# A delta-rule attention and an MLP on one core: the written order of the first five steps is replaced

## The chip, the core and the metric

The kernel runs on one core of a Trainium2 chip. The core has five engines with an instruction queue each: TensorE (PE, matrix products), VectorE (DVE), ScalarE (ACT), GpSimd (POOL) and SyncE (SP, which here only issues DMAs). Each engine works through its own queue in the order in which the instructions were written; a semaphore holds an instruction until what it needs is done, and everything behind it on that engine then waits too. The metric is the device time of one execution in microseconds; smaller is better. The kernel before took 668.8 us (median of three: 668.42, 668.8 and 674.51).

## The reference

The first half is a delta-rule recurrence for 4 batches and 8 heads of width 48 over 768 positions; the second an MLP over the 3072 resulting rows of 384, with 2048 hidden units and a hard-swish.

```python
k_n = k / (np.linalg.norm(k, axis=-1, keepdims=True) + 1e-06)
for t in range(S):
    y[:, :, t] = np.einsum('bhd,bhde->bhe', q[:, :, t], state)
    v_old = np.einsum('bhde,bhd->bhe', state, kt)
    state = state + bt[:, :, :, None] * np.einsum('bhd,bhe->bhde', kt, vt - v_old)
...
x = np.ascontiguousarray(attn_out.transpose(0, 2, 1, 3)).reshape(B * S, H * D)
h = x @ w_in
g = h * np.clip(h + 3.0, 0.0, 6.0) / 6.0
return g @ w_out
```

`w_in` (384 x 2048) and `w_out` (2048 x 384) arrive in 64-bit floats, so they have to be converted on the chip.

## The kernel before

**Steps.** The 768 positions are cut into 24 steps of 32. A step treats 4 batches x 32 positions on the 128 partitions, for all 8 heads. Steps are joined in groups: step 0 alone, then 1 to 4, 5 to 8 and so on. Two steps make a block of 256 rows for the MLP.

**One step t, in the kernel's names.** `prep` (word `p`): normalized keys `kb` (L510, POOL), transposes of keys and queries (`pt`, L524, PE), their copy to `KQ` (L532, ACT), the products of keys with keys and queries (`sc`, L547, PE), and the two masked products `L` and `LB` (L558, DVE). `norms` (`n`): squares (L407 on ACT, L409 on POOL), sum (L413), root (L417) and reciprocal, for `kb`. `mask` (`m`, L486) and `scaled` (`b`, L498): products with beta on POOL.

A triangular system has to be inverted for each step. Step 0 has it by products (`x0`, L596 to L656, DVE, PE and ACT by turns). Steps 1 to 4 have theirs by a substitution on DVE (`i1`: transpose `A` at L469, then pairs of small products L730 and L735, transpose to `X` at L473), which yields two halves for each step, joined by `x1` to `x4` (L694 to L710, products `pi` at L684). Steps 5 to 8 have it by the longer substitution `i2` (L469, L759, L764, L473).

`chain` (`h`) is the recurrence: state products `ks` (L806, PE), `R` (L901, L909, DVE), `pz` (L827, PE), its copy to Z (L927, ACT), state products `su` (L938, PE), the new state (L956, DVE). `output` (`y`): `y` from `ks` (L843 on ACT, L819 on DVE), `py` (L827, PE), sum (L863, DVE; L861 on ACT for step 0), transpose `yt` (L873, PE) and copy to `xT` (L877, ACT).

**Weights.** `w` loads one of 16 chunks of raw weights, 768 KB each (L331, SP); the first 8 are of `w_in`, the last 8 of `w_out`. `a` is one of the four scale steps of a chunk on ACT (L356), `c` one of its three conversions on DVE (L378, L383, L389). The chunks share a few raw buffers, so a later load waits until an earlier chunk has been read.

**MLP.** `ua` and `ub` are the projections of the two halves of block 0 (`ph`, L994), `u` the units of the later blocks (`ph` again, and `po` at L1155); `ra`, `rb`, `ru` are the first half of the activation on ACT (L1001), `ga`, `gb`, `gu` the second on DVE (L1004). `e` copies a finished `po` out. A projection needs `xT` and the converted chunks of `w_in`; `po` needs `g` and `w_out`.

**What sets the order.** `ORDER` is a string of words, one for each piece of such work; `x0*3` stands for three pieces. `do` runs the generator that a word names up to its next `yield`, and so the instructions of that piece are written next, on whichever engines they belong to. `k`, `q`, `v` and `B` issue one load each (keys, queries, values, beta; 48 KB each, L168, L180, L193), `z` and `s` settings. When the string has been worked off, steps 5 to 23 follow by a fixed plan in a loop, which the change doesn't touch. `needs` and `ring` only assert that an order is possible and pick buffers in PSUM; semaphores come from the data.

Of the kernel before, what the change touches and what calls it, by code (L numbers as in the profile page):

```python
# [19 lines left out]


ORDER = """
k*2 B*3 k*2 n0 k*2 z B s*2 n0*6 k*2 q*2 n1 q n1 q w k p0 z*3 k n1*2 k*2 n1*2 z p0*2 s k p0*3 a k a
m0 a n2 m1 p0 x0*2 w q x0 n1 x0*3 c*2 n2 a k s p1*2 a s*2 k q s*2 x0 n2 k*2 c x0 n2 x0 w q a*4 q
p1 n2 k*2 a x0 m2 p1 c*2 p1 n2*3 b1 q b0 s p1 x0 q w x0 n2 q*2 c*3 x0 n4 k p1 k p2*2 x0*2 a*2 c
a*2 q*3 a*2 w v p3*2 q x0 q n4 p2*2 c p2 v c n4*2 a*3 z v n4 c a m3 v c p2 n4*2 q p2 k c b2 h0 c
h0 w a*2 h0 p4*2 a*2 m4 p3 q*4 h0 q k w p4*2 c*5 v*2 p3 k p3*3 k*2 p4*2 v*2 p4 m6 k a w a w i1*3 k
i1*7 a i1*2 a i1*2 v i1*2 k b3 k y0 c y0*3 ua*2 ra*2 i1*3 w v ga v a*3 i1*2 ua i1 h1 i1 q w ua ra
ua i1 ra*2 ga i1 k ua a*2 ra ga i1 ga ua ra ua ra i1 ga i1*4 ua ga n5 x1*2 k x1 c a ra v a*2 ga x2
k*2 ga*2 ua*2 x1 ra*2 x1*2 ua h1*2 n5 k ga c ra ga*2 h1 c y1*2 ua ra w ga ua ra x2 n5 ga y1*2 ua  # L30
ra ga h1 v*3 n5*2 k y1*2 ua a ra x2 ub*2 a n5 rb*2 h1 x3 ga c*2 w a h2 y2 v gb ub rb gb x2 gb ub*2
n5*2 b4 rb n5 x2*2 h2 gb rb gb m5 a n5*2 ub rb gb v c q*2 v q*5 n5 ub n5 rb gb h2 y2 c h2 q ub
y2*2 rb ub p5 b5 h2 rb gb*2 a*2 x3 p5 ub y2*2 k p5*2 h2 rb h3 p5 gb h3 ub*2 q rb gb rb gb ub a x3
p6 v c x4 x3 rb gb ub p7 rb gb y3 c*2 v c p7*2 y3 v p7*2 b6 x3 q x3 ub h3 a p6*2 c p5*2 rb gb k m7
w p6 h3 u p6 k*2 q*3 a*2 y3 a p6 c y3 v y3*2 u n9 v k q a c a c*2 u*2 ru gu w k a*2 c a*2 x4 c*2
ru p7 a gu k u a*2 p7 p6 m8 u*3 a k u*2 k h3 w ru*2 a*2 gu*2 x4 c*2 x4 k c*2 a p8 k a*2 u ru k h3
u*2 h4 ru a b8 gu k gu y4 p8*3 u h4 k*2 c q k*9 q u p8*2 k ru k*2 gu k c n9 q u q*2 p8 k*2 b7 n9*2
x4 i2 u x4 q i2*2 q ub ru gu u rb gb i2*2 h4*2 u*2 i2 ru i2*6 y4 i2 gu i2*7 u i2 ru gu i2 u*3 ru
i2*4 gu ru i2*2 v i2 c gu u*3 a u ru c i2 u*2 i2 gu i2*3 q i2*5 y4 n9 i2 e*2 n9*2 i2*4 q i2 y4 e
n9 u ru i2*3 u h4 i2 ru*2 gu h4 u n9 i2*2 u i2 e i2*6 y4 u k n9*3 u gu i2 y4 n9 i2 p9 q i2*2 gu  # L40
"""


# [1493 lines left out]
```

## Time and profile before

| | |
|---|---|
| times of three runs | 668.42, 668.8, 674.51 us |
| profiled execution | 670.31 us, span 668.6 us |
| PE busy | 635.9 us (95%) |
| DVE busy | 488.6 us (73%) |
| ACT busy | 272.7 us (41%) |
| POOL busy | 203.5 us (30%) |
| moved from and to HBM | 26.84 and 4.72 MB |

The page gives busy time and instruction counts of each engine, then the span in 40 slices of 16.7 us, where a digit is the busy share in tenths; the row PEclk is the clock that PE was granted. A table of stages gives the same in us for chosen stretches. The timeline has one row for each run of equal instructions: start, length, engine, line and operation, and in brackets how long the engine was idle before and what ended that.

### The profile page before, as it was taken

The page shows a single profiled execution, that of the slowest core. Times are in us where ns is not written, and L with a number is a line of the kernel's source. Part 1 is how long each engine was busy: PE and PEld are TensorE (multiplying, and loading weights), DVE is VectorE, ACT ScalarE, POOL GpSimd, SP SyncE. Part 2 cuts the span into 40 slices and gives each one's busy share as a digit, 9 for nine tenths or more (in the row PEclk, how much of TensorE's full clock was granted, in tenths as well). Part 3 has the DMA queues.
Part 4 walks back from the last instruction along what each step waited for, and adds up shares of the span by engine and source line. Part 5 has one row for each costly group of instructions (what it writes and reads, how often), then busy time and mean ns, then how long its engine had stood idle before and what let it go on. Part 6 is the DMA issues. An engine that isn't in the chain of part 4 may idle for free.

```text
span 668.6 us, 26778 instructions
## 1 busy us (share of the span) xinstructions
PE 635.9 (95%) x11768; PEld 578.1 (86%) x11768; DVE 488.6 (73%) x1146; ACT 272.7 (41%) x532; POOL 203.5 (30%) x320
## 2 busy tenths in 40 slices
PE   2659899999999999999999999999999999999997
PEld 2548787776689988988999999999999999999997
DVE  5889686798545687747988858988758998456353
ACT  5887579432143132232244244244244144153250
POOL 6531032002511130463164255064052241331330
PEclk9778899999999999999999999999999999999999
DMA  7888146302041030031030030020020020010000
GB/s 175 203 205 223 57 94 169 65 13 46 18 84 21 3 73 2 2 76 35 3 70 7 3 70 5 3 61 3 3 50 2 2 50 2 17 24 1 26 1 24
DMA packets 88500, 33.29 MB, mean 50 GB/s; under 512 B 80160, under 2 KB 83232, under 8 KB 88384
## 3 DMA queue, kind: packets, MB, share of 16 engines
q1 hardware_dynamic: 88128, 31.29, 21.1%
q8 instruction: 92, 1.51, 1.0%
q10 hardware_dynamic: 256, 0.30, 0.2%
q14 instruction: 24, 0.20, 0.1%
HBM read 26.84 MB, written 4.72 MB: 47 GB/s over the span
## 4 chain that ended last, share of the span: by engine, by line
PE 90%; DVE 3%; DMA 3%; SPq 1%; issue 1%; ACT 1%; ACTq 0%; DVEq 0%
PE po L1219 28%; PE ph L1065 21%; PE ph L994 16%; PE po L1155 6%; PE ks L806 4%; PE pz L827 3%; PE py L827 3%; PE pt L524 3%; PE su L938 3%; PE sc L547 2%; DMA spare<-in_moe_w_in_dram 2%; PE yt L873 1%; SPq L168 1%; PE pi L684 1%; DMA w_out<-in_moe_w_in_dram 1%
## 5 line engine op out<-in xcount | busy, mean ns | idle before, releaser
L1065 PE MATMUL ph<-xT,w_in 128*128 128x128 f32 x784 | 122.9, 278 | 0.0
L994 PE MATMUL ph<-xT,w_in 128*128 128x256 f32 (+1 forms) x576 | 117.5, 355 | 0.6 <-ACT xT L877 0.6
L1219 PE MATMUL po<-w_out,g 128*128 128x192 f32 x640 | 110.6, 326 | 0.0
L994 PEld LDWEIGHTS ph<-xT,w_in 128*128 128x128 f32 x576 | 96.2, 196 | 12.7 <-ACT xT L877 0.8
L1065 PEld LDWEIGHTS ph<-xT,w_in 128*128 128x128 f32 x784 | 103.9, 192 | 1.3 <-ACT KQ L532 0.2
L1219 PEld LDWEIGHTS po<-w_out,g 128*128 128x128 f32 x640 | 104.1, 190 | 0.2
L1030 POOL TENSOR_TENSOR g<-g 128x256 f32<-128x256 f32 x112 | 67.9, 608 | 83.2 <-ACT g L1079 78.8
L1219 PE MATMUL po<-spare,g 128*128 128x192 f32 x480 | 86.7, 332 | 0.0
L1219 PEld LDWEIGHTS po<-spare,g 128*128 128x128 f32 x480 | 77.2, 190 | 1.8
L1001 ACT ACTIVATE g<-ph,halves 128x256 f32<-128x256 f32 (+1 forms) x96 | 41.2, 436 | 75.0 <-PE ph L994 74.9
L1229 POOL TENSOR_TENSOR o<-o,u 128x192 f32<-128x192 f32 x18 | 13.1, 727 | 176.2 <-ACT o L1226 87.0
L1079 ACT ACTIVATE g<-ph 128x512 f32<-128x512 f32 x56 | 33.4, 597 | 80.4 <-PE ph L1065 77.2
L1205 DVE TENSOR_TENSOR g<-g 128x512 f32<-128x512 f32 x80 | 55.7, 717 | 5.6 <-PE po L1219 5.6
L759 DVE TENSOR_TENSOR pr<-A 128x30 f32<-128x30 f32 (+9 forms) x150 | 57.4, 383 | 2.7
L764 DVE TENSOR_TENSOR A<-A,pr 128x30 f32<-128x30 f32 (+9 forms) x150 | 55.7, 371 | 3.7
L1004 DVE SCALAR_TENSOR_TENSOR g<-g,ph 128x256 f32<-128x256 f32 (+1 forms) x96 | 34.7, 370 | 31.6 <-ACT g L1001 31.2
L356 ACT ACTIVATE spare<-spare,places 128x768 uint16<-128x768 uint16 (+1 forms) x56 | 52.5, 942 | 2.6 <-DMA kf<-in_k_dram 1.4
L1094 DVE TENSOR_TENSOR g<-ph,g 128x256 f32<-128x256 f32 x56 | 23.5, 419 | 37.7 <-PE ph L1065 25.6
L1226 ACT ACTIVATE o<-po 128x192 f32<-128x192 f32 x40 | 13.2, 330 | 83.3 <-PE po L1219 83.3
L1108 DVE SCALAR_TENSOR_TENSOR g<-o,g 128x512 f32<-128x512 f32 x56 | 40.9, 730 | 7.0 <-ACT o L1105 6.9
L1155 PE MATMUL po<-w_out,g 128*128 128x384 f32 x128 | 45.2, 491 | 0.0
L510 POOL TENSOR_TENSOR kb<-kf,inv 128x384 f32<-128x384 f32 x24 | 21.3, 891 | 78.3 <-issue 47.4
(141 smaller groups left out, 1005.1 us busy)
## 6 DMA issues: line engine op xcount, KB each, us to landing
kf<-in_k_dram SPq DMA_DIRECT2D x96, 48.0 KB, 3.1
qb<-in_q_dram SPq DMA_DIRECT2D x96, 48.0 KB, 2.8
vf<-in_v_dram SPq DMA_DIRECT2D x96, 48.0 KB, 2.1
out_dram<-o SPq DMA_DIRECT2D x92, 48.0 KB, 1.6
spare<-in_moe_w_in_dram SPq DMA_DIRECT2D x4, 768.0 KB, 5.8
w_out<-in_moe_w_in_dram SPq DMA_DIRECT2D x4, 768.0 KB, 6.3
w_out<-in_moe_w_out_dram SPq DMA_DIRECT2D x4, 768.0 KB, 6.9
spare<-in_moe_w_out_dram SPq DMA_DIRECT2D x4, 768.0 KB, 5.4
```

The costliest lines, as they stand in the source:

```text
L356: nc.scalar.activation(out=z, in_=z if n else d.bitcast(I16)[:, :, :, 3], func=func, bias=places[:, n : n + 1], scale=scale,)
L759: nc.vector.tensor_tensor(out=pv, in0=A[:, j + 1 :, j].unsqueeze(2).to_broadcast([n, w, j]), in1=A[:, j, 0:j].unsqueeze(1).to_broadcast([n ...
L764: nc.vector.tensor_tensor(out=A[:, j + 1 :, 0:j], in0=A[:, j + 1 :, 0:j], in1=pv, op=ALU.subtract)
L827: nc.tensor.matmul(ps[rows(place(b)), D * h : D * h + D], lhsT=m(h)[rows(b)], rhs=z[rows(b), D * at(h) : D * at(h) + D], start=True, stop= ...
L994: nc.tensor.matmul(ph[:, cols], lhsT=w_in[:, s, f * 128 : (f + 1) * 128], rhs=xT[:, s, cols], start=(s == 0), stop=(s == NKT - 1),)
L1001: nc.scalar.activation(out=g, in_=ph, func=ACTF.Relu, bias=half, scale=1.0 / 6.0)
L1030: nc.gpsimd.tensor_tensor(out=out, in0=a, in1=b, op=op)
L1065: nc.tensor.matmul(ph[:, n], lhsT=w, rhs=x, start=start, stop=stop, skip_group_check=True)
L1108: nc.vector.scalar_tensor_tensor(out=g, in0=r, scalar=1.0, in1=g, op0=ALU.min, op1=ALU.mult)
L1155: nc.tensor.matmul(pos[c][:], lhsT=gs[blk, f // 2][:, f % 2, c * P : (c + 1) * P], rhs=w_out[:, f, :], start=(f == 0), stop=(f == NFC - 1),)
L1205: nc.vector.tensor_tensor(out=A(f, *out, 4), in0=A(f, *a, 4), in1=A(f, *b, 4), op=op)
L1219: nc.tensor.matmul(ps[n][:], lhsT=A(f - f % 2, *a)[:, f % 2], rhs=b[:, f], start=(f == 0), stop=(f == HF - 1),)
```

## The change

Only the string `ORDER` is replaced (it is one line longer, so that line numbers of the changed kernel are one higher). It has 782 words in both kernels, and each word equally often. Its description says that the order of the first five steps on all engines was made anew by a longer search, in a model corrected on a trace, with three settings averaged.

```diff
 ORDER = """
-k*2 B*3 k*2 n0 k*2 z B s*2 n0*6 k*2 q*2 n1 q n1 q w k p0 z*3 k n1*2 k*2 n1*2 z p0*2 s k p0*3 a k a
-m0 a n2 m1 p0 x0*2 w q x0 n1 x0*3 c*2 n2 a k s p1*2 a s*2 k q s*2 x0 n2 k*2 c x0 n2 x0 w q a*4 q
-p1 n2 k*2 a x0 m2 p1 c*2 p1 n2*3 b1 q b0 s p1 x0 q w x0 n2 q*2 c*3 x0 n4 k p1 k p2*2 x0*2 a*2 c
-a*2 q*3 a*2 w v p3*2 q x0 q n4 p2*2 c p2 v c n4*2 a*3 z v n4 c a m3 v c p2 n4*2 q p2 k c b2 h0 c
-h0 w a*2 h0 p4*2 a*2 m4 p3 q*4 h0 q k w p4*2 c*5 v*2 p3 k p3*3 k*2 p4*2 v*2 p4 m6 k a w a w i1*3 k
-i1*7 a i1*2 a i1*2 v i1*2 k b3 k y0 c y0*3 ua*2 ra*2 i1*3 w v ga v a*3 i1*2 ua i1 h1 i1 q w ua ra
...
+k*4 B z B k*3 n0 s k n0 B n0 B n0*4 n1*3 q*2 n1 s*2 n1*3 q*2 w*2 z q p0*2 k m0 k*4 p0*3 z*3 p0 a*3
+z p0 x0*3 w x0*2 a*3 c*2 a p1 b0 c s x0*2 k*2 n2 a b1 c*2 q n2 k*2 a p1 n2 k w s k*2 q x0*3 s c n2
+p1 c a x0*2 n2*4 x0 n2 a p2 m2 c q a c*2 x0 k*2 m1 a s b2 p1*2 w n4 q n4 c v*3 k a*4 c p2*2 x0 v
+x0 p3 n4*2 a n4*2 w s*2 p1 q*3 p2 q p2 c n4 h0 p2 c p2 q p1 v h0 q*3 p3 p4 v a*2 v c*2 p3 p4*2 v*2
+h0*2 p3*2 m4 q*4 p4*3 a*2 k*3 m3 c k*2 a k p4 p3*2 i1*2 b4 w q i1*4 y0 i1*5 a y0*2 k y0 k i1*2 b3
+v ua i1 k ra ga i1*10 ua ra ga k h1 i1 a i1 ua a ra ga w ua ra ua ra i1 v ga i1 ua i1 ua*2 i1 ga
...
 """
```

More of the change, by code (lines that the diff above doesn't have):

```diff
@@ L28 @@
-i1*7 a i1*2 a i1*2 v i1*2 k b3 k y0 c y0*3 ua*2 ra*2 i1*3 w v ga v a*3 i1*2 ua i1 h1 i1 q w ua ra
[L29 to L39, printed above, removed]
@@ L40 @@
-n9 u ru i2*3 u h4 i2 ru*2 gu h4 u n9 i2*2 u i2 e i2*6 y4 u k n9*3 u gu i2 y4 n9 i2 p9 q i2*2 gu
+k*4 B z B k*3 n0 s k n0 B n0 B n0*4 n1*3 q*2 n1 s*2 n1*3 q*2 w*2 z q p0*2 k m0 k*4 p0*3 z*3 p0 a*3
[3 more added lines that the diff above has]
+h0*2 p3*2 m4 q*4 p4*3 a*2 k*3 m3 c k*2 a k p4 p3*2 i1*2 b4 w q i1*4 y0 i1*5 a y0*2 k y0 k i1*2 b3
@@ new lines @@
+v ua i1 k ra ga i1*10 ua ra ga k h1 i1 a i1 ua a ra ga w ua ra ua ra i1 v ga i1 ua i1 ua*2 i1 ga
+i1 ra*3 ga x1*2 ua ga c x1 ua n5 x1 ra a*2 q ra a ua w ga m5 x1 ga x3 x1 a ua v h1*2 c*2 ga ra ga
+ra k*2 c y1*2 h1 y1 ua a*3 ua c y1*3 ra*2 h1 ga c*2 q ub ga*2 a n5 ub rb*2 h1 w*2 ua ra ga ua ra
+h2 x2 v q x2 gb v n5 gb n5*2 ub*2 w x3 n5 x2 ga rb v k rb w q ub gb y2 x2 v q n5 rb ub rb n5 a
+gb*3 x2 h2 n5*3 a x2 ub*3 c rb*3 gb x4 gb*2 v h2*2 a c n5*2 p6 q y2 a ub rb y2*2 gb ub*2 rb gb
+y2*2 h2 ub*2 b6 rb x4 q ub rb q gb rb gb v*2 q gb q*4 x3 rb p5 b5 x3 h2 p6 q p6 ub k rb gb*2 p8 p5
@@ new lines @@
+a p5 c x3 p5 h3 x3 k p5 p6*2 k*2 q*2 k*3 p7 p8*2 h3 y3 k p7*2 p8*2 p7*2 k h3*2 q b8 k*2 c k v k y3
+a*2 u y3*2 u y3 a h3 k q c h3 c*3 w m6 y3 u*2 q k*2 q k*3 q ru gu a*3 c p5 p6 k u c*2 w ru gu a
+u*2 a p5 k p6 a*2 q p7 m7 p7 a ru c a gu u v a c k*2 ru h4 gu u c*2 u*2 y4 h4 p8 q c x4 ru n9 gu
+u*3 a*3 k*2 m8 p8 i2*3 w x4*2 ru gu i2*2 a c k x4 u c*2 u v b7 k ru i2 y4 i2 u i2 a i2*3 n9 a gu
+i2*3 ru gu i2 a*2 c*2 i2*4 u*3 ru*2 u gu*2 a c v i2*2 u i2*2 n9*2 u i2 ru u*2 i2 c q*2 i2 u a*2 ru
+gu n9 i2*2 q gu i2*2 h4 i2 k*2 a u c i2*6 h4 i2 u k u k n9 e n9 u k i2 e i2*2 ru gu i2 n9 i2 y4*2
@@ L41 @@
+ru e i2 u i2*3 ru h4 i2*3 e u h4 v gu u gu i2*2 u n9 u y4 n9*2 i2 u i2*4 n9 ru i2 n9 y4 i2*2 gu
+i2*2 p9
 """
```

## The prediction

> **What bounds the kernel now.** First the page: how busy each engine is, and where along the span.
>
> ```profile
> PE 635.9 (95%) x11768; PEld 578.1 (86%) x11768; DVE 488.6 (73%) x1146; ACT 272.7 (41%) x532; POOL 203.5 (30%) x320
> ...
> PE   2659899999999999999999999999999999999997
> ...
> DVE  5889686798545687747988858988758998456353
> ...
> PEclk9778899999999999999999999999999999999999
> DMA  7888146302041030031030030020020020010000
> ```
>
> TensorE (PE) is idle for 668.6 - 635.9 = 32.7 us, nearly all in the first five of the 40 slices, where its clock is also cut and the DMA engines are busiest. The table of stages says it in us (columns: stretch, busy time and instructions of PE, weight loads, DVE, ACT, POOL, then clock, DMA share, GB/s).
>
> ```profile
> 0.00:10.00 10.00, 1.82 (x8) 1.57 (x8) 5.04 (x17) 3.73 (x7) 6.57 (x31) 1.00 0.58 122
> 10.00:20.00 10.00, 5.74 (x219) 4.68 (x222) 7.01 (x19) 6.93 (x10) 6.84 (x15) 1.00 1.07 261
> 20.00:30.00 10.00, 6.28 (x255) 5.03 (x246) 8.45 (x17) 9.84 (x15) 2.38 (x2) 0.68 0.83 200
> 30.00:40.00 10.00, 5.24 (x262) 4.28 (x262) 9.39 (x28) 7.52 (x11) 5.73 (x6) 0.84 0.86 183
> 40.00:50.00 10.00, 5.97 (x210) 5.14 (x209) 8.51 (x14) 9.13 (x13) 2.65 (x6) 0.80 0.76 201
> 50.00:60.00 10.00, 9.42 (x120) 8.91 (x118) 9.31 (x34) 7.24 (x15) 0.00 (x0) 0.83 1.04 270
> 60.00:70.00 10.00, 8.31 (x310) 7.50 (x310) 9.33 (x26) 6.89 (x16) 2.14 (x4) 1.00 0.70 193
> 70.00:80.00 10.00, 8.42 (x214) 7.90 (x213) 5.12 (x13) 6.06 (x12) 0.00 (x0) 0.83 0.02 4
> ```
>
> PE is busy 51.2 of the first 80 us, so 28.8 us of idle lie there; the remaining 3.9 us are the tail. From 80 to 600 us the list of waits has none of PE's. So until about 50 us VectorE (DVE, 8.5 to 9.4 of 10) and ScalarE (ACT, up to 9.8 of 10) set the pace, and then PE. The list of PE's waits (us in total, times, longest) and four rows of the timelines name the places: the waits whose cause the profile calls "issue", ACT's y of step 0, DVE's first inverse, PE's first projection, and the last chunk of w_out on PE.
>
> ```profile
> PE su L938 <- issue: 4.2, 2, 2.3
> PE sc L547 <- ACT KQ L532: 3.7, 4, 1.7
> ...
> PE sc L547 <- issue: 1.0, 2, 0.6
> ```
> ```profile
> 49.04 0.47 ACT L861 ACTIVATE y<-py 128x384 f32<-128x384 f32 x1
> ```
> ```profile
> 47.48 1.93 DVE L469 STREAM_TRANSPOSE A<-L 128x1024 f32<-128x1024 f32 x1
> ```
> ```profile
> 50.70 3.90 PE L994 MATMUL ph<-xT,w_in 128*128 128x128 f32 x18 [0.58 <-ACT xT L877]
> ```
> ```profile
> 145.07 2.74 PE L1155 MATMUL po<-w_out,g 128*128 128x384 f32 x8
> ```
>
> 50.70 is when the first projection starts: before it PE is busy for about 25 us and idle for 25.5. Between it and 80 us only 3.3 us are idle.
>
> **The change, part by part.** Both orders have 782 words and the same number of each, so nothing is added or removed: every instruction and every DMA is moved, not bought. On PE the two programs differ in the first 1614 of 6018 matmuls and are equal from there (about 165 us on). As PE does not wait between 80 and 600 us, the change is worth the PE idle it takes from or adds to the first 165 us, and no more.
>
> I compare by running sums: in the written order of each engine I add the median duration of each instruction's row (PE's at full clock), and note how much stands ahead of a milestone (us, before / after, then its time in the trace of before):
>
> - ACT, first xT copy: 39.0 / 35.3, at 50.15. Four scale steps fewer stand ahead (24, not 28, before y of step 0), at 0.93 each.
> - DVE, A (start of the first inverse): 33.0 / 30.6, at 47.48. Five weight chunks are converted ahead of it, not six.
> - DVE, R of step 1: 48.2 / 45.2, at 63.40; y of step 1: 53.0 / 49.7, at 68.33.
> - PE, first projection: 17.9 / 17.9, at 50.70; state product ks of step 2: 37.1 / 36.5, at 76.86; ks of step 3: 48.5 / 54.7; su of step 3: 74.1 / 62.6; sc of step 8 done: 85.0 / 79.8; po of the last w_out chunk: 104.7 / 104.7, at 145.07.
> - DVE, second A: 94.1 / 87.2, at 127.86; last chunk converted: 108.4 / 109.2 ahead of it, at 142.59; second X: 125.2 / 125.2, at 160.05.
>
> *Start of the projection.* Between 20 and 50 us ACT is mostly full, so 3.7 us less ahead of xT is 3.7 us earlier, if its inputs come. The chunk for which ACT waited 1.37 us at 39.16 is now SP's 42nd transfer, not its 51st, and the values of step 0 the 41st, not the 48th. Against it, the last query piece of step 4 is the 58th, not the 53rd (5 x 0.49 us of issue, 2.5 us), and stands behind a value load that needs pz of step 0 done. An estimate along that path: X of step 0 stands as it did, at 32; the query pieces of step 2, now behind the sixth chunk, land near 33, and pz of step 0 ends at 34.9; the value load and three query pieces go out by 36.9 and land 2.8 later (the page's median), 39.7; transpose and copy (0.6) to 40.3; four scale steps (3.8), y (0.47), yt (0.55) and xT (0.49) to 45.8, 4.9 us earlier than now. DVE's sum alone gives 2.4. I take 4.0, between the two ends and nearest ACT's 3.7, since y is an ACT instruction.
>
> *From there to ks of step 2.* PE's sum is 0.6 smaller. x1's transpose stands 3.4 us less deep on DVE, so PE reaches it about as it does now (wait 0.93). New: pz and py of step 1 are neighbours; before, two blocks of projection (1.5 us) covered the copy of Z. Behind pz, ACT has two relus, the y copy (0.57) and the Z copy (0.49). Bounds: 0 (copies were early) to 1.7 (all four); I take 1.0, and behind py wait two blocks of ph, yt and su.
>
> *Steps 2 to 4.* Between ks and su of step 3 PE now has 7.9 us of work, before 25.6, and DVE between R and the state 3.1, not 20.7. Links and cover: R (0.74 + 0.62) against five groups of transposes (2.2); the Z copy (0.49) against two po (1.3); y (0.55) against two po; xT (0.49) against su (0.81). All are covered by 0.3 us or more: I take 0; with the thinnest cover gone, 0.5 each, 2 in all.
>
> *Second inverse and last w_out chunk.* A needs the mask products of step 8. From the end of sc(8) PE has 24.9 us until it needs the last chunk; DVE has 0.8 + 22.0 + 0.95 = 23.8 us, plus the 0.4 us that it idled between A and this chunk in before. Slack 0.7, where before the conversion ended at 143.5, 1.5 us early. Bounds 0 to 2; I take 0.3. The second X ended 3.1 us before its reader at 165.16 and keeps that, as both move with PE.
>
> *SP and POOL.* Key blocks of later groups move past weights on SP's queue; a late one delays POOL's kb, which PE needs only from the transposes of step 5, at a PE sum of 52. Taken at 0; up to 1.4, ACT's longest wait for a key block.
>
> **Sum:** -4.0 - 0.6 + 1.0 + 0 + 0.3 = -3.3, rounded with the clock to -3.5: a start that comes earlier leaves fewer of the half-clock stretches under it, worth a few tenths. The profiled execution took 670.31 us (span 668.6 and 1.7 around it), so it would take 666.8; it lies 1.5 above the median of the three, 668.8, and from the median the forecast is **665.3 us**.
>
> **The waits named "issue".** PE waited four times for nothing that the profile shows: 0.56 at 26.1, 0.42 at 34.7, 1.86 at 41.0 and 2.34 at 71.6, 5.2 us. Counting PE's instructions in the trace, they begin at numbers 706, 1217, 1473 and 2753, each a multiple of 256 from the next (within one), and the queue "instruction" brings 16 KB packets in these stretches: I read them as instruction refills behind the weight transfers. The long ones are followed by a stretch at half clock (clock 0.54 from 72 to 75 us). My sum leaves them as they are. [...]
>
> **Rivals.**
> 1. *DVE keeps the end of the stage.* DVE idles about 12 us between 87 and 128 us, waiting for sc and for scale steps. If these do not come earlier, the last w_out chunk stays at 143.5 and PE gains only the 1.5 us of slack: 667.3. For it: slack of 0.7 in the sums. Against: sc(8) is 5.2 us earlier in PE's order.
> 2. *All of it.* The start by the full 4.9, 0.6 of order, and the refill at 71.6 (2.34 and the half clock behind it, 3.4 / 2) hidden: -9.5, 659.3. For it: weights are asked for earlier. Against: rows of 32 small matmuls still stand close together there.
> 3. *Slower: refills.* [...] pz, py, yt and su of step 1 now stand closer, and come some 4 us earlier, while the weight transfers, which ran at 183 to 270 GB/s until 70 us, do not. Each further refill costs 2.34 and up to 1.7 of half clock, 4.0. One takes the gain away (669.3), two give 673.4. For it: all four waits lie under such transfers. Against: none fell in the 50 to 62 us stretch at 1.04 DMA share.
> 4. *Nothing moves.* The projection waits for the query pieces, now deeper in SP's queue, and starts at 50.7 again: 668.8.
>
> **Numbers.** Forecast 0.42, rival 1 0.21, rival 2 0.16, rival 3 0.15, rival 4 0.06. The range 659.0 to 671.0 takes in the first two, most of rivals 2 and 4 and the one-refill half of rival 3. A measurement of this kernel tells about 1% (6.7 us) from no change: faster by that needs under 662.1, rival 2 and the best of the forecast, 0.22; slower needs over 675.5, three refills or a stall not seen here, 0.07; within, 0.71.
>
> **What would show it.** First projection at 45.8 to 48.3; first A at 43 to 45; idle of PE in the first 80 us down to about 25; a wait of py for ACT's R of about 1 us; no PE wait between 100 and 165 us beyond 0.5. The forecast is wrong if the projection starts after 50, if waits on "issue" exceed 8 us, or if PE waits for w_out at about 141 us.

## The result and the profile after

The changed kernel took **673.75 us** (median of 20 runs, 670.61 to 677.65) against 669.15 us of the kernel before (20 runs beside them, 666.54 to 674.51): a ratio of **1.0057, 95% interval 1.0036 to 1.0079**, so 2.4 to 5.3 us slower. The forecast was 665.3 us, with a range up to 671.0; it had the wrong sign and the time lies outside the range. Ratios and intervals, here and below, leave out the few executions that took over 1.5% more than the fastest of their kernel; medians are of all.

The profiled execution of the changed kernel took 673.5 us with a span of 671.8. First its page: busy time of PE, then the 40 slices.

```profile
PE 638.2 (95%) x11768; PEld 579.1 (86%) x11768; DVE 485.2 (72%) x1146; ACT 272.2 (41%) x532; POOL 202.6 (30%) x320
...
PE   3668899899999999999999999999999999999997
...
DVE  5779758899545777747878857988748988456353
...
PEclk9988999899999999999999999999999999999999
DMA  7868345502041030032030030020020020010000
```

PE is idle for 671.8 - 638.2 = 33.6 us, before 32.7. So in these two executions the change took no idle time away (in the first 80 us it is 27.5 us, before 28.8), and one thing is new: the eighth slice (117.6 to 134.3 us) shows clock 8, where before nothing behind the fifth slice did. The table of stages has it in us, with the columns of before:

```profile
20.00:30.00 10.00, 4.84 (x179) 4.19 (x179) 8.41 (x17) 6.23 (x10) 4.89 (x7) 1.00 0.97 215
30.00:40.00 10.00, 6.95 (x269) 5.88 (x267) 5.15 (x12) 8.10 (x13) 2.70 (x5) 0.84 0.69 156
40.00:50.00 10.00, 7.19 (x274) 5.66 (x273) 8.11 (x15) 7.21 (x10) 7.01 (x9) 0.84 0.63 145
50.00:60.00 10.00, 9.18 (x119) 8.65 (x118) 9.21 (x36) 5.67 (x13) 0.00 (x0) 0.80 1.06 262
...
120.00:130.00 10.00, 7.84 (x122) 5.51 (x112) 7.52 (x17) 4.14 (x6) 0.00 (x0) 0.83 0.62 148
```

From 120 to 130 us PE is busy for 7.84 us at clock 0.83, under weight loads that moved 184 GB/s from 110 to 120 us and 148 here (before: 102 and 80, PE busy throughout, clock 1.00). The list of PE's waits names what stands there (us in total, times, longest):

```profile
PE pi L597 <- issue: 3.4, 2, 3.0
PE pt L525 <- DMA qb<-in_q_dram: 3.3, 2, 3.0
PE ph L995 <- issue: 2.2, 1, 2.2
...
PE sc L548 <- issue: 1.2, 1, 1.2
...
PE su L939 <- issue: 1.0, 1, 1.0
...
PE ks L807 <- issue: 0.7, 1, 0.7
...
PE py L828 <- ACT R L928: 0.6, 1, 0.6
```

Two entries are new against before: the waits on "issue" add up to 8.9 us (before 5.2), one of them in `ph` at 122.9, in a stretch where PE had not waited at all; and PE waits 3 us for a query piece from memory. The rows that answer to those shown of before:

```profile
47.98 1.94 DVE L470 STREAM_TRANSPOSE A<-L 128x1024 f32<-128x1024 f32 x1
48.62 0.49 ACT L862 ACTIVATE y<-py 128x384 f32<-128x384 f32 x1 [0.63 <-PE py L828]
...
50.64 0.58 PE L995 MATMUL ph<-xT,w_in 128*128 128x128 f32 x1 [0.58 <-ACT xT L878]
...
147.86 1.45 PE L1156 MATMUL po<-w_out,g 128*128 128x384 f32 x4
```

The projection starts at 50.64, before at 50.70: of the 4 us expected there, nothing came in this execution. DVE's first inverse starts at 47.98, where 43 to 45 was expected. The last chunk of `w_out` is first read at 147.86, before at 145.07. Where the time went, stage by stage of the two profiled executions (change in us, from the starting times of the named rows):

| stage | before | after | change |
|---|---|---|---|
| up to the first projection | 50.70 | 50.64 | -0.1 |
| from there to `ks` of step 2 | 26.16 | 23.40 | -2.8 |
| from there to `po` of the last chunk | 68.21 | 73.82 | +5.6 |
| from there to `pz` of step 5 | 20.09 | 20.09 | 0.0 |
| from there to the end | 503.44 | 503.85 | +0.4 |

The loss is in the third row, where PE was the bound and lost nothing before. It is made up of 0.6 of work that moved behind `ks` of step 2 (PE's running sums: 37.1 and 36.5 ahead of it), 0.7 for the wait in `ks` at 75.9, 2.15 for the wait at 122.9, and 1.35 for the half clock that starts in it (122.2 to 125.6 by the clock's own records, of which PE was busy 2.7; an estimate that takes work at half clock to last twice as long: the five `ph` from 122.90 take 2.29 us, the six at 117.43 took 1.46): 4.8 of 5.6. The other 0.8 is not accounted for.

### The profile page after: what moved, and what is told of

The parts are those of the page before. It is cut to its first block, busy times and chain, and to the rows that moved or that the text cites. A ratio compares the mean times of both kernels' runs of the same rounds, so it can differ in the third digit from the quotient of the medians.

```text
span 671.8 us, 26777 instructions
## 1 busy us (share of the span) xinstructions
PE 638.2 (95%) x11768; PEld 579.1 (86%) x11768; DVE 485.2 (72%) x1146; ACT 272.2 (41%) x532; POOL 202.6 (30%) x320
## 4 chain that ended last, share of the span: by engine, by line
PE 89%; DMA 4%; SPq 2%; DVE 2%; issue 1%; ACT 0%; POOL 0%; ACTq 0%; DVEq 0%; POOLq 0%
PE po L1220 28%; PE ph L1066 20%; PE ph L995 16%; PE po L1156 6%; PE ks L807 3%; PE pz L828 3%; PE py L828 3%; PE su L939 3%; PE pt L525 3%; PE sc L548 2%; DMA qb<-in_q_dram 2%; DMA w_out<-in_moe_w_in_dram 1%; PE yt L874 1%; SPq L169 1%; PE pi L685 1%
## 5 line engine op out<-in xcount | busy, mean ns | idle before, releaser
L995 PE MATMUL ph<-xT,w_in 128*128 128x256 f32 (+1 forms) x576 | 117.3, 355 | 2.7 <-issue 2.2
L1095 DVE TENSOR_TENSOR g<-ph,g 128x256 f32<-128x256 f32 x56 | 23.5, 419 | 37.5 <-PE ph L1066 26.6
L1106 ACT ACTIVATE o<-g,halves 128x512 f32<-128x512 f32 x56 | 40.5, 723 | 10.3 <-DVE g L1109 5.4
```

Source lines behind the costliest of these rows:

```text
L995: nc.tensor.matmul(ph[:, cols], lhsT=w_in[:, s, f * 128 : (f + 1) * 128], rhs=xT[:, s, cols], start=(s == 0), stop=(s == NKT - 1),)
L1106: nc.scalar.activation(out=r, in_=g, func=ACTF.Relu, bias=half, scale=1.0 / 6.0)
```

## The wait at 123 us, read from the rows

PE's timeline of the changed kernel, and then that of the kernel before around the same instructions (start, length, idle before in brackets):

```profile
117.43 1.46 PE L995 MATMUL ph<-xT,w_in 128*128 128x256 f32 x6
118.82 0.86 PE L548 MATMUL sc<-KQ 64*32 64x64 f32 x64
119.61 0.73 PE L685 MATMUL pi<-X,sums_in 16*32 16x16 f32 x64
120.26 0.48 PE L995 MATMUL ph<-xT,w_in 128*128 128x256 f32 x1
122.90 2.29 PE L995 MATMUL ph<-xT,w_in 128*128 128x256 f32 x5 [2.15 <-issue]
```
```profile
123.45 1.46 PE L994 MATMUL ph<-xT,w_in 128*128 128x256 f32 x6
124.83 0.86 PE L547 MATMUL sc<-KQ 64*32 64x64 f32 x64
125.62 1.56 PE L994 MATMUL ph<-xT,w_in 128*128 128x256 f32 x6
127.12 0.73 PE L684 MATMUL pi<-X,sums_in 32*32 32x16 f32 x64
```

A group of 64 small matmul records, with as many weight loads, is 128 instructions. In the changed kernel `sc` of step 8 and `pi` of step 4's join stand next to each other: 256 instructions in 1.5 us. In the kernel before a projection block of 1.56 us lies between `sc` and the next `pi`. The wait stands at the 5528th record of PE, matmuls and weight loads counted together, and in the records of the DMA queue "instruction" a 16 KB packet starts at 120.09; PE goes on 2.8 us later. Counted as the prediction counts its four (all of PE's instructions in the trace, those for semaphores too), the seven waits on issue of the changed kernel begin at numbers 449, 706, 1730, 2497, 2754, 3010 and 5569, again multiples of 256 from each other within one. Such waits are what the prediction read as instruction refills, and the places at such distances are called boundaries below. Here one fell in a stretch in which PE of the kernel before was busy throughout (10.00 of the 10 us from 120 to 130). Two observations over all seventeen profiled executions bear this reading out. The wait is at the 5528th to 5530th record in all six that have it, in five different orders. And each of the 86 waits of PE on issue over 0.15 us ends 2.2 to 3.3 us after such a packet has started. Most packets go with no wait of PE: about 25 start in the first 165 us of an execution, and one to eight of them go with a wait.

## The experiments

Every ratio is to runs of the kernel before on the same chip; times are medians, in us. "Start" is the first projection, "`pz`5" the first product of step 5, up to which PE's programs differ, both from the one profiled execution, whose own time stands beside them.

| kernel | median | ratio (95%) | profiled | start | `pz`5 | wait on issue, 115 to 130 us |
|---|---|---|---|---|---|---|
| before | 669.15 | 1 | 670.3 | 50.70 | 165.16 | 0 |
| before, profiled again | | | 669.2 | 51.03 | 162.28 | 0 |
| changed | 673.75 | 1.0057 (1.0036 to 1.0079) | 673.5 | 50.64 | 167.95 | 2.15 |
| changed, profiled again | | | 675.9 | 48.48 | 169.99 | 3.55 |
| new work, old loads | 675.85 | 1.0118 (1.0076 to 1.0161) | 679.6 | 48.38 | 174.59 | 3.71 |
| old work, new loads | 678.71 | 1.0170 (1.0129 to 1.0212) | 677.6 | 56.26 | 169.58 | 0 |
| old start, new rest | 672.16 | 1.0066 (1.0034 to 1.0097) | 676.7 | 52.16 | 171.03 | 3.41 |
| new start, old rest | 669.34 | 1.0038 (1.0007 to 1.0068) | 667.7 | 47.93 | 162.73 | 0 |
| join later | 673.23 | 1.0036 (1.0007 to 1.0066) | 671.2 | 50.15 | 166.17 | 0 |
| join later, profiled again | | | 669.9 | 51.96 | 164.34 | 0 |
| queries first | 672.19 | 1.0038 (1.0014 to 1.0063) | 671.2 | 50.26 | 165.28 | 1.62 |
| both edits | 670.15 | 0.9988 (0.9961 to 1.0015) | 671.3 | 49.04 | 165.68 | 0.43 |
| changed, 232 instructions more | 674.38 | 1.0052 (1.0025 to 1.0080) | 668.8 | 48.25 | 160.54 | 0 |
| the same, profiled again | | | 674.8 | 51.45 | 167.12 | 0 |
| before, 96 instructions more | 681.68 | 1.0173 (1.0137 to 1.0209) | 681.1 | 56.27 | 174.24 | 0 |
| before, 248 instructions more | 671.75 | 1.0024 (0.9986 to 1.0062) | 677.1 | 51.84 | 169.57 | 0 |
| new start, queries first, old rest | 671.15 | 1.0021 (0.9994 to 1.0049) | 670.5 | 48.89 | 163.73 | 0 |

### Loads and work exchanged

First the order of SP's load words was exchanged against that of the other engines' words. The new order of work with the first 110 load words in the old order (an excerpt of the string around the sixth chunk):

```diff
-p2 m2 c q a c*2 x0 k*2 m1 a s b2 p1*2 w n4 q n4 c v*3 k a*4 c p2*2
+p2 m2 c a c*2 x0 m1 a s b2 p1 q*3 k w v*2 k*3 v*2 k w p1 n4*2 c w k a*4 c p2*2
...
```

> The new order on PE, DVE, ACT and POOL, but the first 110 of SP's 160 loads in the old order (beta on ACT's queue likewise). Theory A (the loss comes from the new order of the loads: weights packed earlier hold up PE's instruction refills and the query of step 2): the 3.05 us wait for qb and most of the 3.0 us wait at the sixth product of step 0 go, the first projection starts at 47.5 us or sooner, the time is at most 0.998 of before. Theory B (the loss comes from the new order of the work, which puts dense groups of small matmuls on the refills): the waits on issue stay at 8 us or more and the time at 1.004 of before or more.

The query wait of 3 us and the 3.0 us wait on issue in the first product group are gone and the start came at 48.38, 2.3 us earlier (the changed kernel itself started at 48.48 in its second profile, below, so that this is no sure gain). The waits on issue are 9.0 us in all and the ratio is 1.0118, as theory B has it: the kernel is no faster than the changed one. PE's two waits over 0.5 us in it between 77 and 165 us:

```profile
PE ph L995 <- issue: 3.7, 1, 3.7
PE pt L525 <- DMA qb<-in_q_dram: 2.7, 1, 2.7
```

The first is the wait of the changed kernel at the same place, and longer; the second a later query that the old load order brings too late for the new order of work:

```profile
99.83 1.07 PE L525 MATMUL pt<-ident,qb 128*128 128x128 f32 x8 [2.69 <-DMA qb<-in_q_dram]
```

The reverse, the old order of work with the new loads:

```diff
-a*2 c a*2 q*3 a*2 w v p3*2 q x0 q n4 p2*2 c p2 v c n4*2 a*3 z v n4 c a
+a*2 c a*4 p3*2 x0 n4 p2*2 c p2 c n4*2 a*3 z n4 c a
...
```

> The old order of work with the first 110 of the new order's loads. Theory A: the query of step 2 comes late and refills stall as in the new kernel, first projection after 52 us, 1.004 of before or more. Theory B: within 0.2% of before.

It is slower than the kernel before by 1.7%, so theory B's "within 0.2%" is refuted; but what theory A named isn't the cause either (query wait 1.2 us, waits on issue 1.6 in all). The start lost it: PE's transposes `yt` waited for `y` of step 0.

```profile
54.78 0.90 PE L874 MATMUL yt<-ident,y 128*128 128x128 f32 x3 [6.78 <-ACT y L862]
```

What follows: neither half of the change can be named as the loss by itself. Each order of loads belongs to its order of work, and either mixture is 1.2 to 1.7% slower than the kernel before.

### Start and rest exchanged

The kernels were then cut ahead of the first word `ua` (behind 255 words of the old order, 242 of the new) and joined crosswise. Old start, new rest:

```diff
 i1*3 a i1*2 a i1*2 v i1*2 k b3 k y0 c y0*3
-ua*2 ra*2 i1*3 w v ga v a*3 i1*2 ua i1 h1 i1
+b4 v ua k ra ga i1*8 ua ra ga k h1 i1
...
```

> The old order up to the first projection (255 words), then what is left in the new order. If the loss is made in the start: 1.001 of before or less, and the wait on issue of 2.15 us near 120 us gone or without weight. If it is made in the rest (refill at 120 us under the last loads of w_out, with 3.4 us of half clock behind it): 1.004 or more with that wait still there.

The ratio, 1.0066, can't be told from that of the changed kernel, and the wait is there too:

```profile
124.93 2.07 PE L995 MATMUL ph<-xT,w_in 128*128 128x256 f32 x4 [3.41 <-issue]
```

New start, old rest:

```diff
 i1 y0 i1*5 a y0*2 k y0 k i1*2 b3 v
-ua i1 k ra ga i1*10 ua ra ga k h1
+q c*3 m6 a w a w a*2 i1*3 c ua*2 ra*2 i1
...
```

> The new order up to the first projection (242 words), then what is left in the old order. If the loss is made in the start: first projection at 50 us or later with the waits at 24.8 and 33 us, 1.003 of before or more. If it is made in the rest: 0.999 to 1.001, no wait on issue after 80 us.

It started at 47.93, had `pz`5 at 162.73 (2.4 earlier than the first profile of before, but not earlier than its second, 162.28) and no wait on issue behind 80 us. Its profiled execution was 667.7, yet its median is 669.34 and the ratio 1.0038 (1.0007 to 1.0068), where 0.999 to 1.001 was expected if all the loss is in the rest. What follows: the wait near 123 us belongs to the rest of the new order, whatever start stands ahead of it; but the new start is no gain either, and by its interval it costs something of its own.

### Both kernels profiled again

Since the time of one kernel varies by 7 to 8 us from run to run, both kernels were profiled a second time.

> The changed kernel as it is, profiled a second time, to see which of the waits in its first profile belong to the program and which to one execution. Theory A (boundaries of 256 instructions belong to the program, the lengths of the waits to the traffic): waits on issue at the same places, among them ph at 120 to 126 us, 1.5 to 3.7 us with half clock behind it, and the query of step 2 again landing at 36 (wait about 3). Rival: the wait near 123 was one execution's; it is absent and the time is 671 or less.

The wait is there again, at the same place in the block of `ph` and longer, and half clock from 122.2 to 129.0, starting in it. PE's timeline of that execution:

```profile
118.15 0.86 PE L548 MATMUL sc<-KQ 64*32 64x64 f32 x64
118.94 0.73 PE L685 MATMUL pi<-X,sums_in 16*32 16x16 f32 x64
119.60 0.48 PE L995 MATMUL ph<-xT,w_in 128*128 128x256 f32 x1
123.63 2.29 PE L995 MATMUL ph<-xT,w_in 128*128 128x256 f32 x5 [3.55 <-issue]
```

The query wait came again too (2.84, at 34.1, not at 36), but the wait of 3.0 us at 27.8 was 0.57 here, and the start 48.48.

> The kernel before as it is, profiled a second time, on the chip of the other looks of this call. Theory A: waits on issue at 26, 35, 41 and 71 us again, each 0.4 to 2.5, none between 100 and 165 us, first projection at 50 to 52. Rival: the waits move about from one execution to the next, and one near 100 to 130 us can come up here too.

The kernel before again had nothing between 100 and 165 us and started at 51.03. Of its four waits on issue those at 35 and 41 us came again (0.21 and 1.72), those at 26 and 71 did not; 1.9 us in all in place of 5.2. So in these executions the *places* went with the program and the *lengths* with the execution, and under 80 us two of the four waits were gone. From the first projection to `pz`5 the kernel before took 114.5 and 111.3 us, the changed kernel 117.3 and 121.5: in both executions the loss lies there.

### The join moved behind two units

The smallest edit that parts `sc` from `pi`: the first `x4` goes behind the next two `u`.

```diff
-u*2 y4 h4 p8 q c x4 ru n9 gu u*3 a*3
+u*2 y4 h4 p8 q c ru n9 gu u*2 x4 u a*3
```

> The changed kernel with one word moved: the first x4 (products pi of step 4's join) goes behind the next two u, so that after sc of step 8 PE has a projection block and a po block before the 32 small products pi. Nothing else in the order changes, loads included. Theory A (instruction refills): in the changed kernel sc, pi and the head of the next ph use up a block of 256 PE instructions within 2.7 us, and the wait of 2.15 us at 122.9 and the half clock behind it (3.4 us, of which PE is busy 2.7, so 1.35 lost) are the price. With 4.4 us of large products between them the wait falls under 0.3, no half clock near 122 to 126, and the time falls by 2.15 + 1.35 = 3.5, to 670.2 and a ratio to before of about 1.001. Theory B (the last w_out loads and their conversion, which go out 10 to 13 us later than before, hold PE): the products are not the cause, the time stays at 673 to 674 and PE waits as long somewhere between 118 and 150 us.

PE's timeline of that kernel has 3 us of large products between the two groups, and no wait:

```profile
119.81 0.86 PE L548 MATMUL sc<-KQ 64*32 64x64 f32 x64
120.59 1.56 PE L995 MATMUL ph<-xT,w_in 128*128 128x256 f32 x6
121.99 1.45 PE L1156 MATMUL po<-w_out,g 128*128 128x384 f32 x4
123.38 0.73 PE L685 MATMUL pi<-X,sums_in 16*32 16x16 f32 x64
```

PE waited for nothing over 0.6 us between 77 and 165 us, though the last loads went out as late: theory B (late loads hold PE) is refuted for this wait. The time is another matter: 670.2 was expected, the median is 673.23, the ratio 1.0036 (1.0007 to 1.0066), which isn't shown to be below that of the changed kernel. The same kernel profiled again:

> The changed kernel with the join products pi of step 4 behind the next two u, a second look: its first profile (671.2) had no wait near 123, but its median, 673.2, lies only 0.5 under that of the changed kernel. Theory A: no wait near 118 to 126 again; what a typical execution loses then lies in the first 80 us, where the start (50.15 in the first look), the query wait (4.7) and waits on issue vary by several us. Rival: the wait has moved to a place nearby and comes back in this execution with 2 us or more between 100 and 165 us.

Again no wait there. Both profiled executions (671.2 and 669.9) are shorter than the median, so what a typical run of this kernel loses was not caught in them; the query wait was 4.7 and 4.4 us, the start 50.15 and 51.96.

### Queries ahead of the sixth chunk

The query pieces of step 2 stand behind the sixth weight chunk on SP's queue in the changed kernel. SP's timeline (its issues; `w_out` is the raw buffer here):

```profile
25.69 0.31 SPq L181 DMA_DIRECT2D qb<-in_q_dram  x1
...
29.51 0.93 SPq L332 DMA_DIRECT2D w_out<-in_moe_w_in_dram  x1
31.50 2.28 SPq L181 DMA_DIRECT2D qb<-in_q_dram  x5
```

The first piece goes out at 25.69, the other three from 31.50 on, and PE's transposes of the query wait until 36.40:

```profile
36.40 0.64 PE L525 MATMUL pt<-ident,qb 128*128 128x128 f32 x4 [3.05 <-DMA qb<-in_q_dram]
```

One word was moved:

```diff
-a n4*2 w s*2 p1 q*3 p2 q
+a n4*2 s*2 p1 q*3 w p2 q
```

> The changed kernel with one word moved: the load of the sixth weight chunk goes behind the last three query pieces of step 2, three pieces later on SP's queue; all else as in the changed kernel. My failed term: I had the queries landing at 33; they landed at 36.4 and held PE's transposes for 3.05 us. Theory A: the wait goes to under 1 us, the projection starts at 48 to 49 in place of 50.6, and the end moves by less than that, 0.5 to 2 us, since the wait at 122.9 stays (671.5 to 673.2). Rival: the sixth chunk, issued 2 us later, holds its conversion and all weights behind it, the first projection stays at 50 to 51 and the time at 673.5 to 675.

The wait went from 3.05 to 0.4, as expected, and the time came into the expected stretch. But the start was 50.26, as the rival had it: four waits on issue, 0.8 us at 25.8, 0.55 at 31.1, 1.33 at 36.65 and 0.42 at 46.2, 3.1 in all, stood in its place. SP's timeline shows a second hold-up, further along the same path: the four value loads behind the query pieces were not all out until 37.5, and the four query pieces behind them went out from 37.59 on.

```profile
33.92 3.62 SPq L194 DMA_DIRECT2D vf<-in_v_dram  x4
37.59 3.25 SPq L181 DMA_DIRECT2D qb<-in_q_dram  x4
```

Here `pz` of step 0 had ended at 34.85, where the prediction put it; PE's transposes of the last of these query pieces began at 42.13. The wait near 123 was 1.62.

### Both edits

```diff
-a n4*2 w s*2 p1 q*3 p2 q
+a n4*2 s*2 p1 q*3 w p2 q
...
-u*2 y4 h4 p8 q c x4 ru n9 gu u*3 a*3
+u*2 y4 h4 p8 q c ru n9 gu u*2 x4 u a*3
```

> The changed kernel with both edits: the first x4 behind the next two u, and the sixth weight chunk's load behind the query pieces of step 2. Theory A: the two waits are separate, so both are gone: no wait on the query over 1 us, none near 123, projection start 48 to 50.3, median 1.5 to 3.5 under the changed kernel, 670 to 672. Rival: what is removed comes back as waits on issue elsewhere, median 673 or more.

**Ratio 0.9988 (0.9961 to 1.0015)**, 670.15 us: the loss is gone. Against the changed kernel that is 0.9988 / 1.0057 = 0.993, 4.6 us, and the intervals of the two don't overlap. PE's waits of this kernel between 77 and 165 us:

```profile
PE ph L995 <- DVE g L1005: 0.6, 1, 0.6
PE pi L685 <- issue: 0.4, 1, 0.4
PE su L939 <- issue: 0.4, 1, 0.4
PE py L828 <- issue: 0.2, 1, 0.2
```

Where 2 to 3.6 us stood, 0.4 is left: the boundary now lies inside the moved `pi`, with the wait of 0.43 that ends at 123.37. The query wait was not fully gone here (2.2 us, at 42.1, for the next step's pieces), against the expectation. The kernel can't be told from the one before: no kernel of this study is shown to be faster than that.

### Where the boundaries fall, with the order untouched

The last question is whether the count of instructions does it, and not the order. Small products of the identity, written to a tile that the first transposes then overwrite, were put ahead of PE's work, in time in which PE waits for its first keys. The kernel before with 24 of them:

```diff
             pt = psM.tile([128, NP, P], FP32, name="pt", tag=slot["pm"])
+            for _ in range(24 if t == j == 0 else 0):
+                nc.tensor.matmul(
+                    pt[0:32, 0, 0:32], lhsT=ident[0:32, 0:32], rhs=ident[0:32, 0:32],
+                    start=True, stop=True,
+                )
             for p in range(NP):
```

> The kernel before, order untouched, with 24 of the same small products ahead of the first transposes: 96 PE instructions more, boundaries 96 places earlier. Theory A (refills): by the spacing of the instructions in its trace a boundary then falls into the dense groups at 47 us and at 63.7 and 127.6 us; waits on issue there of 1 to 3 us each, and the total of such waits up from 5.2 to 8 to 10 us, the time from 668.4 to 670.5 to 673, though the order and the loads are those of the kernel before. Rival: where a boundary falls doesn't matter, the time stays within 1 us of the kernel before.

It took 681.68 us, **1.73% more**, 12 us for 24 products that PE works off from 1.95 to 4.71 us, while it waits for its first keys until 8.25. Its two longest waits on issue in PE's timeline:

```profile
54.78 0.90 PE L878 MATMUL yt<-ident,y 128*128 128x128 f32 x3 [5.30 <-issue]
...
108.31 0.65 PE L552 MATMUL sc<-KQ 64*32 64x64 f32 x39 [2.89 <-issue]
```

The direction was right, the size was not (2 to 4.6 us expected), nor the places: a boundary now lies ahead of the transposes `yt`, on which the first projection depends, and the whole MLP waits behind it. Not all of the 5.30 us is the refill's: `y`, which `yt` reads, was ready at 51.20 only (ACT's row 50.73, 0.47 long), so that 3.6 us are left for it. Waits on issue are 10.4 us in all by the profile, before 5.2 and 1.9. From 50 to 60 us PE was busy 4.64 us, at clock 0.50, while the DMA engines moved 289 GB/s. The control has 62 products, 248 instructions, so that boundaries lie 8 instructions from their old places:

```diff
-            for _ in range(24 if t == j == 0 else 0):
+            for _ in range(62 if t == j == 0 else 0):
```

> The kernel before with 62 small products ahead of the first transposes, 248 PE instructions, so that the boundaries of 256 fall 8 instructions later in the program than they did (one block more). It is the control of the run with 24 products, which took 12 us more than the kernel before. Theory A: it is the place of the boundaries, not the added products; with 2.6 times as many of them the places are nearly the old ones, no wait over 2.5 us, time 667 to 671, ratio 0.998 to 1.005. Rival: the products themselves cost the 12 us (an engine held up, a tile kept): 680 or more.

Ratio 1.0024 (0.9986 to 1.0062), as expected; in us it is 0.75 above the stretch named. The longest wait on issue in its profile is 2.41 us, at 73.5, and all of them are 4.7 us. With the 62 products PE's first transposes come at 8.69, 0.5 us later than without (8.18). So it is not the products: 62 cost no more time than the runs can tell, 24 cost 12 us. The changed kernel with 58 of them (in the same place):

```diff
+            for _ in range(58 if t == j == 0 else 0):
```

> The changed kernel with 58 small products of the identity with itself ahead of PE's first transposes, at a time when PE waits for its first keys until 8.3 us; they are written to a PSUM tile that the transposes then overwrite. They add 232 PE instructions, so that every boundary of 256 instructions falls 232 places earlier in the program (24 later than the next one stood), and change no order and no load. Theory A (refills): the boundary inside ph at 122.9 moves 24 instructions on, behind large products, and the wait of 2.15 there falls under 0.8; of the other waits on issue the 3.0 us one at 27.8 shrinks below 0.5, as the group of small products has begun before it. Together waits on issue fall from 8.9 to 3 to 5 us, the time to 669 to 671.5. Theory B (late loads and conversions hold PE): nothing hangs on the count of instructions, the time stays at 673 to 674 with 1.5 us at most for the added products, which lie in idle time.

The wait near 123 was gone, as theory A has it, and its first profile gained 7.4 us up to `pz` of step 5; but the median stayed, 674.38, where 669 to 671.5 was expected.

> The changed kernel with 58 small products ahead of PE's first transposes, a second look. Its first profile was 668.8 us, far under its median of 674.4: it gained 7.4 us by the 4000th matmul against the changed kernel and lost 2.7 of them again behind 200 us, where PE idled 1.9. Theory A: the shifted boundaries fall into dense groups of the later steps too, and a typical execution waits on issue there in total by 3 to 6 us between 200 and 600 us; the time is 672 to 676. Rival: no waits behind 200 us, the time is then made in the first 100 us (a start at 50 or later).

Profiled again, it had waits on issue at 34.4 (3.27) and 72.8 (1.78), 9.2 us in all against 2.7 the first time. Behind 165 us it lost some 2 us both times (the stretch from `pz`5 to the end took 506.6 and 505.9, in the changed kernel 503.9 and 504.2), less than theory A's 3 to 6; most of what differs lay in the first 80 us, as the rival has it (start at 51.45). A shift moves the waits to other places, and only some of them are cheaper.

### The start once more

The changed order up to the cut with the queries first, and the old rest:

```diff
-a n4*2 w s*2 p1 q*3 p2 q
+a n4*2 s*2 p1 q*3 w p2 q
...
-ua i1 k ra ga i1*10 ua ra ga k h1
+q c*3 m6 a w a w a*2 i1*3 c ua*2 ra*2 i1
```

> The changed order up to its 242nd word with the sixth weight chunk's load behind the query pieces of step 2, then the remaining words in the order of the kernel before. Theory A: the start of the changed order without its query wait (3.1 us in the run without this edit), start at 46.5 to 48.5, and the rest of the kernel before, which has no wait behind 80 us: 665.5 to 668.5, faster than both. Rival: the sixth chunk, 2 us later, comes back as a later conversion or the refills of the start take the gain: 668.5 to 671.

The rival won: 671.15, ratio 1.0021 (0.9994 to 1.0049), not to be told from the kernel before. The start was 48.89, and this row of PE's timeline took what it had gained:

```profile
57.55 0.79 PE L995 MATMUL ph<-xT,w_in 128*128 128x128 f32 x2 [4.01 <-DVE g L1005]
```

The projection runs ahead of DVE, which is busy 7.45 of the 8 us from 50 to 58, and waits for its `g`.

## Why the prediction was wrong

**Start, -4.0: failed.** The step that fell first is "the query pieces of step 2 ... land near 33". They landed at 36.4 (wait 3.05), and in the other execution at 34.1 (2.84). The same first 242 words started at 50.64, 48.48, 47.93, 50.15 and 51.96 in five profiled executions, mean 49.8; the old start at 50.70, 51.03 and 52.16, mean 51.3. So the term is about -1.5, and as single starts of one order differ by up to 4 us, not even that is shown. Counting what stands ahead on ACT and DVE said nothing of SP's queue, and my walk along it took the sixth chunk's place for less than it was. Nor is the query of step 2 the only bound: with it ahead of the chunk the start was 50.26, 49.04 and 48.89. The walk's next step, the value load and the query pieces out "by 36.9" and landed at 39.7, failed as well: PE could use the last of these pieces at 42.89 in the first profile of the changed kernel, and still only at 42.13 with the queries first, though `pz` of step 0 then ended when the walk had it. (The walk's own terms add up to 45.6, not to its 45.8.) The walk also had no PE work between the copy and `y`; in the first profile ACT's `y` waited 0.63 us for `py`, behind a wait of PE on issue of 1.25 at 46.79.

**Order up to `ks` of step 2, -0.6: not parted from the refills.** The stage became 2.8 shorter, but 2.34 of wait and its half clock (71.3 to 74.7) stood in it before, and 1.4 of waits now.

**`py` right behind `pz`, +1.0 (0 to 1.7): right within its bounds.** It waited 0.59 and 0.84 us for ACT's `R`.

**Covers of steps 2 to 4, 0: right.** No wait for R, Z, `y` or `xT` between 77 and 165 us. **Last `w_out` chunk, +0.3 (0 to 2): right**; PE didn't wait for it although its load went out at 119.96, 13 us later than before. **Key blocks, 0: right.** PE's only wait for `kb` is the one of 8.3 us at its very start, and that was 8.2 before.

**"My sum leaves them as they are": the second step that failed.** I had counted the four waits, found the distance of 256 instructions, and then carried 5.2 us into the changed kernel unaltered. They were 8.9 and 7.9 us in its two profiled executions. The dear one is that near 123, which I had at nothing ("no PE wait between 100 and 165 us beyond 0.5"). In the five profiled executions with that part of the order as changed it was 2.15, 3.55, 3.41, 3.71 and 1.62, mean 2.9; the half clock that started in it, its length less PE's idle time in it, halved, was 1.4, 2.7, 2.5, 2.3 and 1.7, mean 2.1. Together 5.0 us. With the -1.5 of the start that gives +3.5; the measured ratio is +3.8. This sum is an estimate, not a proof, and that it meets the ratio so nearly is in part luck, as its start term is no larger than its scatter. Two kernels had no wait near 123 in any profile and were not shown to be faster for it: with the join moved the ratio was 1.0036, with the boundaries shifted 1.0052, and neither interval parts it from 1.0057. Only with the join and the queries moved together is the gain shown, and it is not shown how it divides between the two.

**Rivals.** Rival 3 had the kind of wait (one more, 4.0 us each) and rival 4 the start (50.7, from the query pieces deeper in SP's queue). I gave them 0.15 and 0.06 as if only one could happen. In the first profile both did, which by their own prices is 668.8 + 4.0 = 672.8; in the second the start was 48.48 and the wait longer. Two of the prediction's three signs of being wrong came in the first profile, a start after 50 and waits on issue over 8 us, and neither in the second. Rival 3 also looked at the wrong groups: it named `pz`, `py`, `yt` and `su` of step 1, where waits of 0.4 and 1.0 us fell, while the dearest wait, 2.15 and 3.55 us in the two profiles, stood right behind `sc` of step 8 and `pi` of step 4's join. Counting the distance between small groups all along PE's order, as for the waits of before, would have shown two of them side by side at 118.8.

**What stays open.** Whether the late loads (184 and 148 GB/s from 110 to 130 us) were needed for the wait: the loads were not moved alone in that part, since a later chunk can't be loaded before an earlier one has been converted. Why the kernel with the join moved has a median 2 to 3 us above both its profiled executions. And why the shifted kernel, without the wait, is no faster.

## What to carry to other kernels

In this case an order of instructions could not be judged without the places where its boundaries fell: 96 instructions ahead of the untouched order cost 1.73%, 248 nothing that can be told (ratio 1.0024, 0.9986 to 1.0062). When many small matmuls are moved, count 256 instructions, the unit of the distances between the waits of both kernels here, along the engine's new order and look for two boundaries with little work between them; part such groups with large products. As an estimate of "little": in the five long waits near 123 us PE went on 3.6 to 5.7 us after the start of `sc`, and had some 2 us of work for that time. Profile two or more executions before a wait is costed, since here the wait near 123 us kept its place (the 5528th to 5530th record in six executions) and not its length (0.43 to 3.71 us); and a running sum per engine needs a second column, the place of each load in its queue.

## What the runs showed of the hardware

- **Waits of PE went with packets of the queue "instruction".** In seven long waits PE goes on 2.4 to 2.8 us after the 16 KB packet starts on that queue (120.09 to 122.90, 121.27 to 123.63, 122.41 to 124.93, 126.06 to 128.52, 117.15 to 119.77, 52.16 to 54.78, 105.49 to 108.31). In the first profiles of the kernel before and of the changed one the waits lie multiples of 256 instructions apart, within one (before 706, 1217, 1473 and 2753, changed 449 to 5569). Shifting all boundaries by 96 instructions cost 12 us (ratio 1.0173), by 248 nothing that can be told (1.0024). With most packets PE didn't wait (about 25 in the first 165 us, one to eight with a wait), with the others up to 3.7 us each.
- **With the long waits near 123 us came half clock** (granted clock 0.50), 3.4 or 6.8 us long in a stage where PE otherwise ran at 1.00: with the wait of 2.15 us 122.2 to 125.6, with 3.55 us 122.2 to 129.0 (the four `po` from 125.71 took 2.76 us there, the eight at 114.08 only 2.85), with 3.71 us 126.3 to 133.1. In the first profile of the kernel with the join moved, which has no wait there, the products took their time at full clock (six `ph` at 120.59 took 1.56 us, four `po` at 121.99 and 124.03 took 1.45 and 1.56). So a wait of 3.6 us cost some 6.3 by the estimate above. The length of the wait doesn't settle it: in the kernel with new work and old loads PE waited 2.69 us for a query and the clock stayed at 1.00 from 95 to 110 us, while a wait on issue of 1.62 us, that with the queries first, came with half clock (five `ph` from 119.77 took 2.39 us). And in the kernel before the half clock at the wait of 41 us, which by the prediction follows the wait, ran from 37.2 to 44.0, the wait from 39.1 to 41.0.
